# Cached grouped-query attention: scores further ahead of values, K further ahead of V, and weights loaded in row pieces

## The chip, the cores and the metric

The kernel runs on one core of a Trainium2 chip. The metric is the time on the device in microseconds (us), as a median of several runs. Engines are named as in the profile: PE (TensorE, matmuls; its weight loads are PEld), DVE (VectorE), ACT (ScalarE), POOL (GpSimd) and SP (SyncE, which issues nearly all DMAs here). Line numbers (L143) are those of the kernel before, as printed below.

## The reference

Eight sequences with four new tokens each attend to a cache of 2048 positions. There are 32 query heads and 8 key/value heads of 128 elements, so four query heads share one key/value head. All tensors are bf16.

```python
B, Sq, D = 8, 4, 512
Hq, Hkv, Sk, Dh = 32, 8, 2048, 128
q = (x @ wq).reshape(B, Sq, Hq, Dh).transpose(0, 2, 1, 3)
k = jnp.repeat(k_cache, Hq // Hkv, axis=1)
v = jnp.repeat(v_cache, Hq // Hkv, axis=1)
scores = jnp.einsum("bhqd,bhkd->bhqk", q, k) * (Dh ** -0.5)
p = softmax(scores)
o = jnp.einsum("bhqk,bhkd->bhqd", p, v)
return o.transpose(0, 2, 1, 3).reshape(B, Sq, Hq * Dh) @ wo
```

k_cache and v_cache hold 33.6 MB each, wq and wo 4.2 MB each.

## The kernel before

**Units.** The work is cut into 32 units: four pairs of key/value heads (p, outer) times eight sequences (b, inner). A unit needs 1 MB of K and 1 MB of V. Both come as tiles of 128 partitions with 32 chunks of 128 elements; partitions 0 to 63 hold the first head of the pair and 64 to 127 the second. A unit has 32 query columns: eight query heads by four tokens. It is worked on as two halves of 16 chunks, so there are 64 half-units.

**A half-unit's stages.** `transpose_part` (L136 on) turns eight chunks of K with PE against an identity into one PSUM tile `kp`, and DVE copies it to `kt` (ACT in one of four cases). `scores` multiplies 16 chunks of `kt` by the queries into `s_ps`, and ACT writes the exponentials into `probs`, separately for the two heads' partitions; the crossed blocks keep the zeros set at the start. `values` multiplies 16 chunks of V by `probs` into `o_ps`. In the second half of a unit it first sums the probabilities: eight matmuls with `ones` over all 32 chunks into `l_ps` (L178), a reduction on DVE (L186) and a reciprocal (L193); at the end DVE writes `o_ps` times that reciprocal into `oT_all` (L206).

**Reordering and projection.** `shuffle` takes the eight heads of a finished pair, turns them to token order (`nat`), copies, turns them again into the row order in which wo is loaded (`perm`) and copies the result to `oP[p]`. `project` then multiplies `oP` by wo, in two column halves of 256 in two PSUM banks (L270).

**Order.** The order of each engine is the order of the program text (`manual_schedule`); waits are put between engines where data or buffers need them. The loop over steps runs from -2 to 63. Step i does the transposes of half-unit i+2, the scores of i+1 and the values of i. In the first half-unit of a pair's second sequence it also does the whole `shuffle` of the pair before. After a unit's second half the loop issues `load_k(u + 1 + KB)` and `load_v(u + VB)`; K has seven buffers (KB) and V six (VB). The six loads of wo are issued after unit 25's second half, behind the last V. After the loop come `project(0)`, the last `shuffle`, the other projections, two casts (L286, L287) and two stores.

**Loads.** All loads go through SP in the order x, wq (one load of 128 partitions, 32 KB each), K0, K1, V0, K2, V1 and so on: K(u+1) stands directly ahead of V(u). SP holds an issue until the buffer is free and until an earlier load's semaphore can be used again.

Of the kernel before, what the change touches and what calls it, by code (L numbers as in the profile page):

```python
# [7 lines left out]

BF16 = mybir.dt.bfloat16
FP32 = mybir.dt.float32  # L10
EXP = mybir.ActivationFunctionType.Exp


@with_exitstack
def kernel(
# [9 lines left out]
    nc = tc.nc  # L25

    B, Sq, D = x.shape
# [4 lines left out]
    T = B * Sq  # L32
    R = D // 128
    G2 = Hkv // 2
    C = 2 * Sk // 128
    NQ = 2 * rep * Sq
    HC = C // 2
    HP = 2 * rep
    scale = float(Dh) ** -0.5
    NU = G2 * B  # L40
    NH = 2 * NU
    KB = 7
    VB = 6
    WR = HP
    DH = D // 2
    assert Dh == 128 and C == 32 and NQ == 32

    const = ctx.enter_context(tc.tile_pool(name="const", bufs=1))
# [3 lines left out]
    small = ctx.enter_context(tc.tile_pool(name="small", bufs=2))  # L52
    psum_k = ctx.enter_context(tc.tile_pool(name="psum_k", bufs=3, space=bass.MemoryType.PSUM))
    psum_s = ctx.enter_context(tc.tile_pool(name="psum_s", bufs=2, space=bass.MemoryType.PSUM))
    psum_o = ctx.enter_context(tc.tile_pool(name="psum_o", bufs=2, space=bass.MemoryType.PSUM))
    psum_l = ctx.enter_context(tc.tile_pool(name="psum_l", bufs=1, space=bass.MemoryType.PSUM))
# [5 lines left out]
    wq_sb = const.tile([128, R, HqDh], BF16, name="wq_sb")  # L62
    xT_sb = const.tile([128, R, T], BF16, name="xT_sb")
    qT_all = const.tile([128, G2, B, HP, Sq], BF16, name="qT_all")
    oT_all = const.tile([128, Hq, B, Sq], BF16, name="oT_all")
    wo_sb = const.tile([128, G2, WR, D], BF16, name="wo_sb")
    out_sb = [const.tile([T, DH], BF16, name=f"out_sb{i}") for i in range(2)]
    ident = const.tile([128, 128], BF16, name="ident")
    ones = const.tile([128, 128], BF16, name="ones")
    probs = [const.tile([128, C, NQ], BF16, name=f"probs{i}") for i in range(3)]  # L70

    units = [(p, b) for p in range(G2) for b in range(B)]
    ks = [None] * NU
# [2 lines left out]
    def load_k(u):  # L76
        if u >= NU:
            return
        p, b = units[u]
        ks[u] = kpool.tile([128, C, Dh], BF16, tag="k_sb", name="k_sb")  # L80
        nc.sync.dma_start(  # L81
            ks[u][:, :, :],
            k_cache[b, 2 * p : 2 * p + 2].rearrange("g (s c) d -> (g s) c d", c=C),
        )

    def load_v(u):
        if u >= NU:
            return
        p, b = units[u]
        vs[u] = vpool.tile([128, C, Dh], BF16, tag="v_sb", name="v_sb")  # L90
        nc.sync.dma_start(  # L91
            vs[u][:, :, :],
            v_cache[b, 2 * p : 2 * p + 2].rearrange("g (s c) d -> (g s) c d", c=C),
        )

    def load_wo(p, r0, n):
        rows = wo[p * HP * 128 : (p + 1) * HP * 128, :].rearrange("(q r) j -> q r j", r=WR)
        nc.sync.dma_start(wo_sb[:, p, r0 : r0 + n, :], rows[:, r0 : r0 + n, :])

    nc.sync.dma_start(x_sb[:, :], x.flatten_outer_dims())  # L100
    nc.sync.dma_start(wq_sb[:, :, :], wq.rearrange("(p r) n -> p r n", r=R))  # L101
    load_k(0)
    for u in range(VB):
        load_k(u + 1)
        load_v(u)

    make_identity(nc, ident[:])
    nc.vector.memset(ones[:, :], 1.0)
# [9 lines left out]
    for p in range(G2):  # L118
        psq = psum_s.tile([128, HP, T], FP32, tag="s", name="psq")
        for h in range(HP):  # L120
            hh = p * HP + h
            for r in range(R):
# [3 lines left out]
                    rhs=xT_sb[:, r, :],  # L126
# [11 lines left out]
    def transpose_part(i, part):  # L138
        u, hf = divmod(i, 2)
        c0 = hf * HC + part * (HC // 2)  # L140
        kp = psum_k.tile([128, HC // 2, 128], BF16, tag="k", name="kp")
        for c in range(HC // 2):
            nc.tensor.transpose(kp[:, c, :], ks[u][:, c0 + c, :], ident[:, :])  # L143
        k_t = ktpool.tile([128, HC // 2, 128], BF16, tag="kt", name="kt")
        if part == 1 and hf == 1:
            nc.scalar.copy(out=k_t[:, :, :], in_=kp[:, :, :])  # L146
        else:
            nc.vector.tensor_copy(out=k_t[:, :, :], in_=kp[:, :, :])  # L148
        kt[(i, part)] = k_t
# [21 lines left out]
    def values(i):  # L171
        u, hf = divmod(i, 2)
        p, b = units[u]
        pr = probs[u % len(probs)]
        if hf == 1:
            l_ps = psum_l.tile([128, 4, NQ], FP32, tag="l", name="l_ps")
            for c in range(C // 4):
                nc.tensor.matmul(  # L178
                    l_ps[:, :, :],
                    lhsT=ones[:, :],  # L180
                    rhs=pr[:, c * 4 : (c + 1) * 4, :],
                    start=(c == 0),
                    stop=(c == C // 4 - 1),
                )
            l_sb = small.tile([128, NQ], FP32, tag="l_sb", name="l_sb")
            nc.vector.tensor_reduce(  # L186
                out=l_sb[:, :],
                in_=l_ps[:, :, :].rearrange("d c q -> d q c"),
                axis=mybir.AxisListType.X,
                op=mybir.AluOpType.add,  # L190
            )
            r_sb = small.tile([128, NQ], FP32, tag="r_sb", name="r_sb")
            nc.vector.reciprocal(r_sb[:, :], l_sb[:, :])  # L193
        if hf == 0:
            o_ps[u] = psum_o.tile([128, NQ], FP32, tag="o", name="o_ps")
        for c in range(HC):
            cc = hf * HC + c
            nc.tensor.matmul(  # L198
                o_ps[u][:, :],
                lhsT=vs[u][:, cc, :],  # L200
                rhs=pr[:, cc, :],
                start=(cc == 0),
                stop=(cc == C - 1),
            )
        if hf == 1:
            nc.vector.tensor_tensor(  # L206
                out=oT_all[:, p * HP : (p + 1) * HP, b, :],
                in0=o_ps[u][:, :].rearrange("d (h s) -> d h s", h=HP),
                in1=r_sb[:, :].rearrange("d (h s) -> d h s", h=HP),
                op=mybir.AluOpType.mult,  # L210
            )

    oP = [None] * G2

    def shuffle(p):
        nat = psum_l.tile([T, HP, 128], BF16, tag="l", name="nat")
        for h in range(HP):
            nc.tensor.transpose(  # L218
                nat[:, h, :],
                oT_all[:, p * HP + h, :, :].rearrange("d b s -> d (b s)"),  # L220
                ident[:, :],
            )
        nat_sb = small.tile([T, HP * 128 // WR, WR], BF16, tag="nat_sb", name="nat_sb")
        nc.vector.tensor_copy(  # L224
            out=nat_sb[:, :, :].rearrange("t q r -> t (q r)"),
            in_=nat[:, :, :].rearrange("t h d -> t (h d)"),
        )
        perm = psum_l.tile([128, WR, T], BF16, tag="l", name="perm")
        for r in range(WR):
            nc.tensor.transpose(  # L230
                perm[:, r, :],
                nat_sb[:, :, :].rearrange("t q r -> t r q")[:, r, :],
                ident[:T, :T],
            )
        oP[p] = const.tile([128, WR, T], BF16, name=f"oP{p}")
        nc.vector.tensor_copy(out=oP[p][:, :, :], in_=perm[:, :, :])

    for step in range(-2, NH):
        if step + 2 < NH:
            transpose_part(step + 2, 0)  # L240
        if 0 <= step + 1 < NH:
            scores(step + 1)
        if step + 2 < NH:
            transpose_part(step + 2, 1)
        if step < 0:
            continue
        values(step)
        u, hf = divmod(step, 2)
        p, b = units[u]
        if hf == 0:  # L250
            if b == 1 and p > 0:
                shuffle(p - 1)
        else:
            if u == 0:
                load_k(KB)
            load_k(u + 1 + KB)
            load_v(u + VB)
            if u + VB == NU - 1:
                for w in range(G2 - 1):
                    load_wo(w, 0, WR)  # L260
                load_wo(G2 - 1, 0, 4)
                load_wo(G2 - 1, 4, 2)
                load_wo(G2 - 1, 6, 2)

    out_ps = [psum_s.tile([T, DH], FP32, tag="s", name=f"out_ps{i}") for i in range(2)]

    def project(p, r0, n):
        for half in range(2):
            for r in range(r0, r0 + n):
                nc.tensor.matmul(  # L270
                    out_ps[half][:, :],
                    lhsT=oP[p][:, r, :],
                    rhs=wo_sb[:, p, r, half * DH : (half + 1) * DH],
                    start=(p == 0 and r == 0),
                    stop=(p == G2 - 1 and r == WR - 1),
                )

    project(0, 0, WR)
    shuffle(G2 - 1)
    for p in range(1, G2 - 1):  # L280
        project(p, 0, WR)
    project(G2 - 1, 0, 4)
    project(G2 - 1, 4, 2)
    project(G2 - 1, 6, 2)
    o2 = out.flatten_outer_dims()
    nc.vector.tensor_copy(out=out_sb[0][:, :], in_=out_ps[0][:, :])  # L286
    nc.scalar.copy(out=out_sb[1][:, :], in_=out_ps[1][:, :])  # L287
    nc.sync.dma_start(out=o2[:, :DH], in_=out_sb[0][:, :])
    nc.scalar.dma_start(out=o2[:, DH:], in_=out_sb[1][:, :])


# [28 lines left out]
```

## Time and profile before

| | us |
|---|---|
| median of 7 runs | 197.31 |
| lowest, highest | 197.11, 198.26 |
| the profiled run | 196.99 |
| its span in the trace | 195.2 |
| busy in the span: PE, PEld | 152.9, 143.2 |
| busy in the span: DVE, ACT | 97.3, 84.0 |
| HBM read | 75.53 MB, 387 GB/s over the span |
| median time from issue to landing, K and V loads | 20.2 each |

The span is the time between the first and the last instruction in the trace; the run's time holds some 1.8 us more around it. PE and PEld overlap, so their times are not added. A DMA's instruction on SP is short; its bytes move later, and the time to landing is from the issue to the last byte. An issue that lies long in the queue behind others therefore has a long landing time.

### The profile page before, as it was taken

To read this page: it belongs to the slowest core of one execution; us is meant where nothing else is said; L and a number is where in the kernel's file an instruction comes from. 1 tells how busy PE (TensorE), PEld (TensorE's weight loads), DVE (VectorE), ACT (ScalarE), POOL (GpSimd) and SP (SyncE) were. 2 spreads that over 40 slices of the span, in tenths; PEclk is the share of its full clock that TensorE was granted. 3 is DMA by queue.
4 is the path that set the end of the run, shared out by engine and by line. 5 is a ranking of instruction groups with operands and counts; after the bars stand their busy time and mean duration, and the time that the engine had idled before them with its cause. 6 is when DMAs were issued, how large, how long until landed. Compare 5 with 4: busy or idle time off the path is not lost.

```text
span 195.2 us, 7883 instructions
## 1 busy us (share of the span) xinstructions
PE 152.9 (78%) x3588; PEld 143.2 (73%) x3588; DVE 97.3 (50%) x209; ACT 84.0 (43%) x166; POOL 0.7 (0%) x6
## 2 busy tenths in 40 slices
PE   1029887888579869988888789988987798878984
PEld 0029887777479869977777689877877798777873
DVE  4003455555427545655555547655554566545310
ACT  2003654544535515645554535645544265445200
POOL 1000000000000000000000000000000000000000
PEclk9999999999969997999999969999999999999999
DMA  6989999999999999999999999999999999999610
GB/s 222 430 383 430 423 416 418 420 423 413 421 418 420 411 421 421 423 411 420 421 423 413 421 413 425 416 418 415 421 416 418 420 420 416 421 420 408 260 50 7
DMA packets 10401, 76.07 MB, mean 390 GB/s; under 512 B 1184, under 2 KB 1280, under 8 KB 1664
## 3 DMA queue, kind: packets, MB, share of 16 engines
q1 hardware_dynamic: 10320, 75.55, 93.4%
q8 instruction: 28, 0.46, 1.0%
q14 instruction: 5, 0.04, 0.1%
q10 hardware_dynamic: 48, 0.02, 0.0%
HBM read 75.53 MB, written 0.03 MB: 387 GB/s over the span
## 4 chain that ended last, share of the span: by engine, by line
DMA 74%; PE 18%; issue 2%; SPq 1%; ACT 1%; DVE 1%; ACTq 0%
DMA v_sb<-in_v_cache_dram 74%; PE kp L143 6%; PE out_ps L270 4%; PE s_ps L159 3%; PE o_ps L198 3%; PE l_ps L178 2%; DVE nat_sb L224 1%; PE perm L230 1%; SPq L81 1%; PE nat L218 1%; ACT kt L146 1%; ACT probs L165 0%; SPq L91 0%; SPq L101 0%; SPq L100 0%
## 5 line engine op out<-in xcount | busy, mean ns | idle before, releaser
L148 DVE COPY kt<-kp 128x1024 bf16<-128x1024 bf16 x96 | 66.0, 689 | 52.2 <-PE kp L143 42.3
L143 PE MATMUL kp<-ident,k_sb 128*128 128x128 bf16 x1024 | 81.6, 223 | 6.8 <-issue 6.6
L165 ACT ACTIVATE probs<-s_ps 64x256 bf16<-64x256 f32 x128 | 48.4, 378 | 82.3 <-PE s_ps L159 80.8
L143 PEld LDWEIGHTS <-k_sb 128*128 128x128 bf16 x1024 | 60.7, 99 | 8.2 <-issue 7.8
L198 PE MATMUL o_ps<-probs,v_sb 128*128 128x32 bf16 x1024 | 36.1, 177 | 13.9 <-DMA v_sb<-in_v_cache_dram 13.6
L198 PEld LDWEIGHTS <-v_sb 128*128 128x128 bf16 x1024 | 31.8, 96 | 17.5 <-DMA v_sb<-in_v_cache_dram 17.2
L159 PE MATMUL s_ps<-qT_all,kt 128*128 128x32 bf16 x1024 | 39.5, 177 | 2.1 <-ACT kt L146 0.8
L159 PEld LDWEIGHTS <-kt 128*128 128x128 bf16 x1024 | 34.2, 97 | 4.4 <-ACT kt L146 1.1
L146 ACT COPY kt<-kp 128x1024 bf16<-128x1024 bf16 x32 | 32.4, 1012 | 1.7 <-PE kp L143 1.0
L186 DVE TENSOR_REDUCE l_sb<-l_ps 128x32 f32<-128x128 f32 x32 | 9.3, 292 | 24.8 <-PE l_ps L178 24.8
L178 PE MATMUL l_ps<-probs,ones 128*128 128x128 bf16 x256 | 21.3, 228 | 0.6 <-ACT probs L165 0.3
L178 PEld LDWEIGHTS <-ones 128*128 128x128 bf16 x256 | 16.9, 103 | 0.8 <-issue 0.8
L193 DVE RECIPROCAL r_sb<-l_sb 128x32 f32<-128x32 f32 x32 | 11.3, 353 | 1.1
L123 PE MATMUL psq<-xT_sb,wq_sb 128*128 128x32 bf16 x128 | 3.6, 188 | 10.3 <-DMA wq_sb<-in_wq_dram 10.3
L123 PEld LDWEIGHTS <-wq_sb 128*128 128x128 bf16 x128 | 3.5, 104 | 10.4 <-DMA wq_sb<-in_wq_dram 10.4
L206 DVE TENSOR_TENSOR oT_all<-o_ps,r_sb 128x32 bf16<-128x32 f32 x32 | 6.1, 192 | 3.3
L130 ACT ACTIVATE qT_all<-psq 128x256 bf16<-128x256 f32 x4 | 1.5, 385 | 14.0 <-PE psq L123 14.0
L270 PE MATMUL out_ps<-wo_sb,oP 128*32 128x256 bf16 x64 | 7.3, 273 | 0.0
L270 PEld LDWEIGHTS <-oP 128*32 128x32 bf16 x64 | 6.0, 97 | 0.8
L230 PE MATMUL perm<-ident,nat_sb 32*128 32x32 bf16 x32 | 2.7, 212 | 3.1 <-DVE nat_sb L224 3.1
L230 PEld LDWEIGHTS <-nat_sb 32*128 32x128 bf16 x32 | 2.3, 162 | 3.8 <-DVE nat_sb L224 3.8
L224 DVE COPY nat_sb<-nat 32x1024 bf16<-32x1024 bf16 x4 | 2.7, 679 | 4.6 <-PE nat L218 4.6
(17 smaller groups left out, 11.4 us busy)
## 6 DMA issues: line engine op xcount, KB each, us to landing
k_sb<-in_k_cache_dram SPq DMA_DIRECT2D x32, 1024.0 KB, 20.2
v_sb<-in_v_cache_dram SPq DMA_DIRECT2D x32, 1024.0 KB, 20.2
wq_sb<-in_wq_dram SPq DMA_DIRECT2D x1, 4096.0 KB, 12.3
wo_sb<-in_wo_dram SPq DMA_DIRECT2D x3, 1024.0 KB, 21.3
wo_sb<-in_wo_dram SPq DMA_DIRECT2D x1, 512.0 KB, 20.1
wo_sb<-in_wo_dram SPq DMA_DIRECT2D x2, 256.0 KB, 17.3
x_sb<-in_x_dram SPq DMA_DIRECT2D x1, 32.0 KB, 1.7
out_dram<-out_sb SPq DMA_DIRECT2D x1, 16.0 KB, 1.4
```

Source lines behind the costliest of these rows:

```text
L123: nc.tensor.matmul(psq[:, h, :], lhsT=wq_sb[:, r, hh * 128 : (hh + 1) * 128], rhs=xT_sb[:, r, :], start=(r == 0), stop=(r == R - 1),)
L143: nc.tensor.transpose(kp[:, c, :], ks[u][:, c0 + c, :], ident[:, :])
L146: nc.scalar.copy(out=k_t[:, :, :], in_=kp[:, :, :])
L148: nc.vector.tensor_copy(out=k_t[:, :, :], in_=kp[:, :, :])
L159: nc.tensor.matmul(s_ps[:, c, :], lhsT=k_t[:, c % (HC // 2), :], rhs=q2, start=True, stop=True)
L165: nc.scalar.activation(out=pr[rows, hf * HC : (hf + 1) * HC, cols], in_=s_ps[rows, :, cols], func=EXP)
L178: nc.tensor.matmul(l_ps[:, :, :], lhsT=ones[:, :], rhs=pr[:, c * 4 : (c + 1) * 4, :], start=(c == 0), stop=(c == C // 4 - 1),)
L186: nc.vector.tensor_reduce(out=l_sb[:, :], in_=l_ps[:, :, :].rearrange("d c q -> d q c"), axis=mybir.AxisListType.X, op=mybir.AluOpType.add,)
L193: nc.vector.reciprocal(r_sb[:, :], l_sb[:, :])
L198: nc.tensor.matmul(o_ps[u][:, :], lhsT=vs[u][:, cc, :], rhs=pr[:, cc, :], start=(cc == 0), stop=(cc == C - 1),)
L230: nc.tensor.transpose(perm[:, r, :], nat_sb[:, :, :].rearrange("t q r -> t r q")[:, r, :], ident[:T, :T],)
L270: nc.tensor.matmul(out_ps[half][:, :], lhsT=oP[p][:, r, :], rhs=wo_sb[:, p, r, half * DH : (half + 1) * DH], start=(p == 0 and r == 0), st ...
```

## The change

- The loop starts at -7. Step i does the transposes of half-unit i+7, the scores of i+6 and the values of i. `probs` has five buffers, not three.
- The order of loads becomes K0, K1, K2, K3, V0, K4, V1 and so on. A list of loads is walked by `load_ready` after every step, as far as the counts of finished units allow.
- The sums of a unit (`norms`) are made before the second half's values, with two matmuls of 512 columns in place of eight of 128, and a reduction over 16 columns a query in place of four. The final multiplication is a function of its own (`finish`).
- `shuffle` is split: `to_tokens` in the pair's second sequence, `to_wo_rows` in its third. After the loop, `to_tokens(3)` precedes `project(0)` and `to_wo_rows(3)` follows it.
- The projection has one PSUM tile of 512 columns: 32 matmuls in place of 64. Two casts read its halves into one tile, and one store writes the output.
- wq and the first three of the four pairs of wo are each loaded as three DMAs, of partitions 0 to 111, 112 to 119 and 120 to 127.

```diff
+PARTS = [(0, 112), (112, 120), (120, 128)]
...
+    L = 6
+    KA = L // 2 + 1
...
+    LC = 16
...
-    probs = [const.tile([128, C, NQ], BF16, name=f"probs{i}") for i in range(3)]
+    probs = [const.tile([128, C, NQ], BF16, name=f"probs{i}") for i in range(L // 2 + 2)]
...
-        nc.sync.dma_start(wo_sb[:, p, r0 : r0 + n, :], rows[:, r0 : r0 + n, :])
+        for lo, hi in PARTS if n == WR else [(0, 128)]:
+            nc.sync.dma_start(wo_sb[lo:hi, p, r0 : r0 + n, :], rows[lo:hi, r0 : r0 + n, :])
...
-    nc.sync.dma_start(wq_sb[:, :, :], wq.rearrange("(p r) n -> p r n", r=R))
-    load_k(0)
-    for u in range(VB):
-        load_k(u + 1)
-        load_v(u)
+    for lo, hi in PARTS:
+        nc.sync.dma_start(wq_sb[lo:hi, :, :], wq.rearrange("(p r) n -> p r n", r=R)[lo:hi])
+    loads = []
+    for u in range(NU + KA):
+        if u < NU:
+            loads.append(("k", u))
+        if u >= KA - 1 and u - KA + 1 < NU:
+            loads.append(("v", u - KA + 1))
+    loads.reverse()
+
+    def load_ready(nk, nv):
+
+        while loads:
+            kind, u = loads[-1]
+            if u >= (nk + KB if kind == "k" else nv + VB):
+                return
+            loads.pop()
+            (load_k if kind == "k" else load_v)(u)
+
+    load_ready(0, 0)
...
+    def norms(u):
+        pr = probs[u % len(probs)]
+        l_ps = psum_l.tile([128, LC, NQ], FP32, tag="l", name="l_ps")
+        for c in range(0, C, LC):
+            nc.tensor.matmul(
+                l_ps[:, :, :],
+                lhsT=ones[:, :],
+                rhs=pr[:, c : c + LC, :],
+                start=(c == 0),
+                stop=(c + LC == C),
+            )
...
-    for step in range(-2, NH):
-        if step + 2 < NH:
-            transpose_part(step + 2, 0)
-        if 0 <= step + 1 < NH:
-            scores(step + 1)
-        if step + 2 < NH:
-            transpose_part(step + 2, 1)
...
+    for step in range(-L - 1, NH):
+        i, j = step + L + 1, step + L
+        if i < NH:
+            transpose_part(i, 0)
+        if 0 <= j < NH:
+            scores(j)
+        if i < NH:
+            transpose_part(i, 1)
         u, hf = divmod(step, 2)
...
+        if step >= 0:
+            p, b = units[u]
+            if hf == 1:
+                norms(u)
+            values(step)
+            if hf == 1:
+                finish(u)
+            elif p > 0 and b == 1:
+                to_tokens(p - 1)
+            elif p > 0 and b == 2:
+                to_wo_rows(p - 1)
+        load_ready(min((i + 1) // 2, NU), max((step + 1) // 2, 0))
+        if step == NH - 1 - 2 * VB:
+            assert not loads
+            for w in range(G2 - 1):
+                load_wo(w, 0, WR)
+            load_wo(G2 - 1, 0, 4)
+            load_wo(G2 - 1, 4, 2)
+            load_wo(G2 - 1, 6, 2)
...
+        for r in range(r0, r0 + n):
+            nc.tensor.matmul(
+                out_ps[:, :],
+                lhsT=oP[p][:, r, :],
+                rhs=wo_sb[:, p, r, :],
+                start=(p == 0 and r == 0),
+                stop=(p == G2 - 1 and r == WR - 1),
+            )
+
+    to_tokens(G2 - 1)
     project(0, 0, WR)
-    shuffle(G2 - 1)
+    to_wo_rows(G2 - 1)
...
+    nc.vector.tensor_copy(out=out_sb[:, :DH], in_=out_ps[:, :DH])
+    nc.scalar.copy(out=out_sb[:, DH:], in_=out_ps[:, DH:])
+    nc.sync.dma_start(out=out.flatten_outer_dims(), in_=out_sb[:, :])
```

More of the change, by code (lines that the diff above doesn't have):

```diff
@@ L43 @@
     VB = 6
+    L = 6
+    KA = L // 2 + 1
     WR = HP
     DH = D // 2
+    AX = mybir.AxisListType.X
+    LC = 16
+    ADD = mybir.AluOpType.add
     assert Dh == 128 and C == 32 and NQ == 32
@@ L66 @@
     wo_sb = const.tile([128, G2, WR, D], BF16, name="wo_sb")
-    out_sb = [const.tile([T, DH], BF16, name=f"out_sb{i}") for i in range(2)]
+    out_sb = const.tile([T, D], BF16, name="out_sb")
+    oP = [const.tile([128, WR, T], BF16, name=f"oP{p}") for p in range(G2)]
     ident = const.tile([128, 128], BF16, name="ident")
     ones = const.tile([128, 128], BF16, name="ones")
-    probs = [const.tile([128, C, NQ], BF16, name=f"probs{i}") for i in range(3)]
+    probs = [const.tile([128, C, NQ], BF16, name=f"probs{i}") for i in range(L // 2 + 2)]
     units = [(p, b) for p in range(G2) for b in range(B)]
@@ L174, in values @@
         pr = probs[u % len(probs)]
[L175 to L193, printed above, removed]
         if hf == 0:
@@ L204, in values, with finish, to_tokens @@
             )
[L205 to L210, printed above, removed]
-            )
-    oP = [None] * G2
-    def shuffle(p):
+    r_sbs = {}
+    def norms(u):
[8 more added lines that the diff above has]
+                stop=(c + LC == C),
+            )
+        l_sb = small.tile([128, NQ], FP32, tag="l_sb", name="l_sb")
+        nc.vector.tensor_reduce(
+            out=l_sb[:, :], in_=l_ps[:, :, :].rearrange("d c q -> d q c"), axis=AX, op=ADD
+        )
+        r_sb = small.tile([128, NQ], FP32, tag="r_sb", name="r_sb")
+        nc.vector.reciprocal(r_sb[:, :], l_sb[:, :])
+        r_sbs[u] = r_sb
+    def finish(u):
+        p, b = units[u]
+        nc.vector.tensor_tensor(
+            out=oT_all[:, p * HP : (p + 1) * HP, b, :],
+            in0=o_ps[u][:, :].rearrange("d (h s) -> d h s", h=HP),
+            in1=r_sbs[u][:, :].rearrange("d (h s) -> d h s", h=HP),
+            op=mybir.AluOpType.mult,
+        )
+    nats = {}
+    def to_tokens(p):
         nat = psum_l.tile([T, HP, 128], BF16, tag="l", name="nat")
@@ L227, in shuffle, with to_wo_rows @@
         )
+        nats[p] = nat_sb
+    def to_wo_rows(p):
         perm = psum_l.tile([128, WR, T], BF16, tag="l", name="perm")
@@ L231, in shuffle @@
                 perm[:, r, :],
-                nat_sb[:, :, :].rearrange("t q r -> t r q")[:, r, :],
+                nats[p][:, :, :].rearrange("t q r -> t r q")[:, r, :],
                 ident[:T, :T],
             )
-        oP[p] = const.tile([128, WR, T], BF16, name=f"oP{p}")
         nc.vector.tensor_copy(out=oP[p][:, :, :], in_=perm[:, :, :])
-    for step in range(-2, NH):
-        if step + 2 < NH:
-            transpose_part(step + 2, 0)
-        if 0 <= step + 1 < NH:
-            scores(step + 1)
-        if step + 2 < NH:
-            transpose_part(step + 2, 1)
-        if step < 0:
-            continue
-        values(step)
-        u, hf = divmod(step, 2)
[L249 to L263, printed above, removed]
@@ L265 @@
-    out_ps = [psum_s.tile([T, DH], FP32, tag="s", name=f"out_ps{i}") for i in range(2)]
-    def project(p, r0, n):
[L268 to L276, printed above, removed]
+    for step in range(-L - 1, NH):
[6 more added lines that the diff above has]
+            transpose_part(i, 1)
+        u, hf = divmod(step, 2)
+        if step >= 0:
+            p, b = units[u]
+            if hf == 1:
[15 more added lines that the diff above has]
+            load_wo(G2 - 1, 6, 2)
@@ L278 @@
+    out_ps = psum_s.tile([T, D], FP32, tag="s", name="out_ps")
+    def project(p, r0, n):
+        for r in range(r0, r0 + n):
[5 more added lines that the diff above has]
+                stop=(p == G2 - 1 and r == WR - 1),
+            )
+    to_tokens(G2 - 1)
     project(0, 0, WR)
-    shuffle(G2 - 1)
+    to_wo_rows(G2 - 1)
     for p in range(1, G2 - 1):
@@ L284 @@
     project(G2 - 1, 6, 2)
[L285 to L289, printed above, removed]
+    nc.vector.tensor_copy(out=out_sb[:, :DH], in_=out_ps[:, :DH])
+    nc.scalar.copy(out=out_sb[:, DH:], in_=out_ps[:, DH:])
+    nc.sync.dma_start(out=out.flatten_outer_dims(), in_=out_sb[:, :])
 _INS = ['x', 'k_cache', 'v_cache', 'wq', 'wo']
```

## The prediction, made before the changed kernel ran

> **What bounds the kernel now.** I read the page's slices and DMA queues first, because the kernel loads 75.5 MB and computes little with them.
>
> ```profile
> GB/s 222 430 383 430 423 416 418 420 423 413 421 418 420 411 421 421 423 411 420 421 423 413 421 413 425 416 418 415 421 416 418 420 420 416 421 420 408 260 50 7
> q1 hardware_dynamic: 10320, 75.55, 93.4%
> q8 instruction: 28, 0.46, 1.0%
> ```
>
> From the second slice to the 37th the loads run at about 420 GB/s without a hole, then thin out over two slices (260, 50). A table of stretches of the tail (columns: stretch, length, busy us and count of PE, PEld, DVE, ACT, POOL, clock, DMA share, GB/s) shows how:
>
> ```profile
> 152.00:178.00 26.00, 22.55 (x560) 21.48 (x561) 15.61 (x33) 12.84 (x26) 0.00 (x0) 1.00 1.01 419
> 182.00:184.00 2.00, 1.70 (x32) 1.47 (x30) 0.84 (x3) 0.40 (x2) 0.00 (x0) 1.00 0.56 226
> 184.00:186.00 2.00, 1.54 (x19) 1.26 (x16) 0.42 (x1) 0.00 (x0) 0.00 (x0) 1.00 0.49 190
> 186.00:188.50 2.50, 2.18 (x23) 1.99 (x24) 0.55 (x2) 0.00 (x0) 0.00 (x0) 1.00 0.16 57
> 188.50:192.40 3.90, 3.83 (x36) 3.16 (x33) 0.25 (x1) 0.03 (x1) 0.00 (x0) 1.00 0.00 0
> ```
>
> For 4 us half of the 16 DMA engines have nothing left (share 0.56, 0.49). The completion counts in the trace say the same load by load: wq's 16 counts came within 0.28 us of one another, those of the last wo load at 181.8 (first) to 188.3 (last). Eight are within 2.2 us of the first, eight are 4.7 to 6.5 us behind it. The late eight fell back in jumps of about 1.5 us, as many as there are packets on queue q8: instruction blocks, each taking about 1.07 us.
>
> Third, the view of wo's loads and the chain that ended last (start, length, what):
>
> ```profile
> L98 SPq DMA_DIRECT2D wo_sb<-in_wo_dram x6: 327/327/328, 159.5 to 171.9; - x6
> DMA to landing us min/median/max: 16.4/20.7/21.3
> ```
> ```profile
> 151.98 0.05 issue
> ...
> 183.25 1.85 PE out_ps L270 x16
> 185.10 0.46 PE nat L218 x8
> 185.56 0.02 issue
> 185.58 0.69 DVE nat_sb L224
> 186.27 0.05 issue
> 186.32 0.67 PE perm L230 x8
> 186.99 5.36 PE out_ps L270 x48
> 192.34 0.02 issue
> 192.37 0.36 ACT out_sb L287
> ```
>
> The last wo load lands at 171.9 + 16.4 = 188.3, but PE ends the projection at 192.34. From 151.98, where a V landing last released it, to that end, PE waits for no load: it carries transposes, scores and values that could have run earlier. Two things end late: PE 4.0 us after the last byte, and the last byte 6.5 us after the fastest DMA engine.
>
> Fourth, the waits of the load queue:
>
> ```profile
> SPq L81 <- DMA wq_sb<-in_wq_dram: 8.3, 1, 8.3
> ```
>
> The tenth load (K4) was issued at 13.51, when wq, the second, landed: a load waits for the one eight before it, so eight are in flight.
>
> [...] The trace has only loads of 128 rows or 32, all with 16 counts; it shows no 8-row load. [...]
>
> **The change part by part.** One DMA engine moves its 64 KB of a 1 MB load in 2.48 us (V issues in the steady state are 2.48 apart): 25.8 KB per us.
>
> *Schedule.* Scores run six half-units ahead of values instead of one, and K(u+3) is queued just ahead of V(u) where K(u+1) was. Per unit PE's chain pieces are 4 x 0.46 (transposes) + 2 x 0.39 (scores) + 0.45 (sums) + 2 x 0.39 (values) = 3.85 us, and a unit's two loads take 4.96. From 14.7 us on PE has 3.6 (wq product) + 32 x 3.85 + 3 x 1.1 (reorderings) = 130 us of work, so some 33 us of slack before the last V lands at 177.9. When it lands, all transposes and scores are done; PE owes two value groups and a sum, 1.2 us, then nat 0.46, project(0) 1.8, perm 0.67, and the middle pairs at 8 x 0.223 = 1.8 us against 2.48 between landings of wo. PE then waits for wo. After its last landing two matmuls stay. This removes the backlog; what is late next is the last wo byte.
>
> Load queue: V(u+6) needs values(u) finished, which now also follows the first half of K(u+4), landing just after V(u). By the eight-load rule it waits for V(u+2), three landings (7.4 us) after K(u+4), against some 2.5 us of PE work, so 5 us cover it. K(u+10) needs only K(u+3) transposed and has more. If that cover went, each late issue would cost its lateness once. At the start K0 to K3 come before V0; PE does a unit of transposes and scores in 2.6 us, the load in 2.48, so it falls behind by under 1 us and regains it later.
>
> *Row sums:* 8 matmuls of 128 columns become 2 of 512, the same columns, 0.45 us. The reduction reads 512 instead of 128 elements: between 0.29 (no change) and 4 x 0.292 = 1.17 us; I take 0.65: 384 elements more at the 0.95 ns an element that the memset of probs shows (485 ns for 512). It follows no V and finishes beside values; DVE is busy 97 of 195 us. Two more memsets of probs (0.49 each) end before 4 us, under the wait for wq. Cost nothing.
>
> *Reordering split:* the waits of perm for DVE's copy (0.78 each) are filled with a step's other work. Nothing on the path, since PE has slack.
>
> *Projection:* 64 matmuls at 5.36/48 = 0.112 become 32 at 0.223: the same 7.1 us, but only 0.45 after the last landing. Casting two halves of one bank: [...] the casts run between together (0.41) and in turn (0.8); the trace, with two banks, does not show it. I take 0.6. One store of 32 KB instead of two of 16: 1.4 us as now.
>
> *Row pieces:* wq as 112 + 8 + 8 rows gives eight engines nine rows of 32 KB and eight engines seven; three 1 MB loads of wo do so with rows of 8 KB. So 32 + 24 = 56 KB move from one half of the engines to the other: 2.17 us. If the relieved half is the late one, it ends at 6.55 - 2.17 = 4.4 and the other at 2.15 + 2.17 = 4.3: the last byte comes at 188.3 - 2.17 = 186.1. Eight more issues of 0.33 us fit beside the queue's waits. The small loads also take places among the eight in flight: at the end they hold about 1.9 MB, 4.6 us, enough. wq itself ends 1.2 us later, which the slack covers. PE loses 192 + 32 matmuls with their loads, so 6728 instructions, two blocks fewer; I count nothing for that.
>
> *Sum.* 186.1 + 0.1 (release) + 0.45 (two matmuls) + 0.6 (casts) + 2.47 (from the end of ACT's cast at 192.73 to the end of the span, 195.2) = 189.7, that is 5.5 less. The profiled run took 196.99 around its span: 191.5. The median of the seven runs is 0.3 above that run: 191.8; with the terms rounded I take **191.9**. Its own range is 190.5 to 193.5, from the casts, the fetched blocks and a last landing within 1 us.
>
> **The rivals.**
>
> *Relief without effect.* The pieces cost what they save (issue and small transfers), and the last landing stays at 188.3: 2.17 later, 194.1. For it: no run here shows what eight small loads cost the engines beside their bytes. Against: nine rows remain nine rows of time.
>
> *Relief on the wrong half.* If the late eight are mixed among the low numbers, a late engine gets 2.17 more: landing at 190.5, 4.4 after the forecast's, and 196.3, near no change. For it: no view numbers the engines. Against: the late eight form one clean group, as eight neighbours would.
>
> [...]
>
> That the schedule does not do what it says (PE still behind at 178) has 33 us of slack against it; I give it nothing of its own.
>
> **How the numbers follow.** Forecast 0.58; relief without effect 0.10; wrong half 0.07[...]. What 0.3% of 197.3, 0.6 us, cannot tell from no change is only part of the wrong half. Faster 0.58 + 0.10 + 0.04 = 0.72; same 0.03; slower 0.25. The range goes from 190.2 past the second and third case[...] up to 200.5 it leaves 0.2 out.
>
> **What would show it.** Right: the chain ends wo landing, two matmuls of 512 columns, casts; PE waits for wo near the end; the DMA share drops steeply from 1 to 0; scores wait for no V. Wrong: wq landing after 16 us, or a DMA share near 0.5 for several us at the start or the end[...]; SP waiting for PE during the steady state (buffers); PE still without waits after 178.

## The result, and the profile after

The changed kernel takes 219.25 us (median of 12 runs, 218.05 to 220.17); the kernel before took 197.52 beside it. The ratio is 1.110, with a 95% interval of 1.108 to 1.112. The forecast was 191.9 and its range ended at 200.5, so the time lies far outside, on the other side of the kernel before. The span of the profiled run went from 195.2 to 217.4 us. Line numbers from here on are those of the kernel whose view is shown.

The slices of the changed kernel (GB/s in 40 equal slices, here 5.4 us each) and its DMA queues:

```profile
GB/s 199 235 258 128 83 365 422 416 422 421 418 421 414 417 414 422 417 421 419 419 416 424 416 421 422 416 419 411 422 414 427 411 424 411 255 216 219 216 91 8
...
q1 hardware_dynamic: 10384, 75.57, 94.4%
q8 instruction: 26, 0.43, 0.8%
```

The middle is as before, about 418 GB/s. Two stretches are new: five slices at the start with 83 to 258 GB/s, where wq is loaded, and four at the end with 216 to 255, where wo is. The bytes are the same. The table of stretches shows both (columns as in the prediction's: stretch, length, five engines, clock, DMA share, GB/s):

```profile
15.00:20.00 5.00, 0.00 (x0) 0.00 (x0) 0.00 (x0) 0.00 (x0) 0.00 (x0) 1.00 1.04 134
20.00:25.00 5.00, 0.00 (x0) 0.00 (x0) 0.00 (x0) 0.00 (x0) 0.00 (x0) 1.00 0.95 98
...
195.00:200.00 5.00, 2.11 (x43) 1.35 (x39) 1.69 (x4) 0.00 (x0) 0.00 (x0) 0.50 0.95 202
```

The DMA share stays near 1 while 98 GB/s are moved. The DMA engines are not out of work, as half of them were at the end of the kernel before; each packet takes longer. A row of wq, one packet of 32 KB, takes 1.21 us in the trace of the kernel before; here it takes 2.13 in the load of 112 rows (medians) and 3.6 to 5.2 in the two of 8 rows. So of the two signs of trouble at the start or the end that the forecast named, wq's late landing came (28.8 us, and the sign was 16), but the share of 0.5 did not. PE has nothing to do until wq is there. The view of wq shows when its product starts (min/median/max ns, first and last start), 28.9 us where before it was 13.5:

```profile
L147 PE MATMUL psq<-xT_sb,wq_sb x128: 176/188/190, 28.9 to 32.3; 128*128 128x32 bf16 x128
```

The view of wo's loads, now twelve, gives the last landing as 205.5 + 7.3 = 212.8, against 188.3:

```profile
L107 SPq DMA_DIRECT2D wo_sb<-in_wo_dram x12: 271/302/1343, 175.6 to 205.5; - x12
...
DMA to landing us min/median/max: 7.3/15.4/23.5
```

The end of the chain that ended last:

```profile
175.58 26.06 DMA wo_sb<-in_wo_dram
201.64 0.02 issue
201.66 8.78 DMA wo_sb<-in_wo_dram
210.44 0.14 issue
210.57 3.63 PE out_ps L301 x16
214.20 0.02 issue
214.23 0.42 DVE out_sb L317
214.65 0.02 issue
214.67 0.36 ACT out_sb L318
```

As forecast, PE's backlog has left the chain: from 175.6 on it consists of wo's loads, the last 16 matmuls and the casts, with no transpose. But it spends 34.9 us on the loads. ACT's cast also waits for DVE's: it begins at 214.67, when DVE's has ended, while in the kernel before DVE's ran 0.41 us from 192.1 and ACT's began at 192.37. The two now read one PSUM tile and write one output tile; which of these makes ACT wait is not shown.

### The profile page after: what moved, and what is told of

The parts are those of the page before. It is cut to its first block, busy times and chain, and to the rows that moved or that the text cites. A ratio compares the mean times of both kernels' runs of the same rounds, so it can differ in the third digit from the quotient of the medians.

```text
span 217.4 us, 7343 instructions
## 1 busy us (share of the span) xinstructions
PE 150.1 (69%) x3334; PEld 132.1 (61%) x3364; DVE 107.6 (50%) x211; ACT 83.9 (39%) x166; POOL 0.7 (0%) x6
## 4 chain that ended last, share of the span: by engine, by line
DMA 92%; PE 5%; issue 0%; SPq 0%; DVE 0%; ACT 0%
DMA k_sb<-in_k_cache_dram 68%; DMA wo_sb<-in_wo_dram 16%; DMA wq_sb<-in_wq_dram 8%; PE kp L167 2%; PE out_ps L301 2%; PE o_ps L203 1%; PE s_ps L183 1%; PE l_ps L217 0%; PE nat L246 0%; DVE out_sb L317 0%; SPq L109 0%; ACT out_sb L318 0%; SPq L99 0%; SPq L89 0%
## 5 line engine op out<-in xcount | busy, mean ns | idle before, releaser
L167 PE MATMUL kp<-ident,k_sb 128*128 128x128 bf16 x1024 | 79.1, 223 | 16.8 <-DMA k_sb<-in_k_cache_dram 16.8
L167 PEld LDWEIGHTS <-k_sb 128*128 128x128 bf16 x1024 | 59.9, 99 | 19.1 <-DMA k_sb<-in_k_cache_dram 19.0
L203 PEld LDWEIGHTS <-v_sb 128*128 128x128 bf16 x1024 | 34.4, 97 | 16.5 <-DMA v_sb<-in_v_cache_dram 7.2
L183 PE MATMUL s_ps<-qT_all,kt 128*128 128x32 bf16 x1024 | 38.4, 177 | 5.9 <-ACT kt L170 4.9
L225 DVE TENSOR_REDUCE l_sb<-l_ps 128x32 f32<-128x512 f32 x32 | 21.9, 683 | 9.3 <-remote 4.2
L217 PE MATMUL l_ps<-probs,ones 128*128 128x512 bf16 x34 | 13.7, 414 | 1.5 <-issue 0.4
L301 PE MATMUL out_ps<-wo_sb,oP 128*32 128x512 bf16 x32 | 9.0, 437 | 2.8 <-DMA wo_sb<-in_wo_dram 2.8
L301 PEld LDWEIGHTS <-oP 128*32 128x32 bf16 x32 | 3.2, 106 | 7.6 <-DMA wo_sb<-in_wo_dram 3.6
L217 PEld LDWEIGHTS <-ones 128*128 128x128 bf16 x64 | 5.0, 100 | 0.1
L266 DVE COPY oP<-perm 128x256 bf16<-128x256 bf16 x4 | 1.2, 291 | 5.7 <-PE perm L261 5.7
```

The costliest lines, as they stand in the source:

```text
L183: nc.tensor.matmul(s_ps[:, c, :], lhsT=k_t[:, c % (HC // 2), :], rhs=q2, start=True, stop=True)
L203: nc.tensor.matmul(o_ps[u][:, :], lhsT=vs[u][:, cc, :], rhs=pr[:, cc, :], start=(cc == 0), stop=(cc == C - 1),)
L217: nc.tensor.matmul(l_ps[:, :, :], lhsT=ones[:, :], rhs=pr[:, c : c + LC, :], start=(c == 0), stop=(c + LC == C),)
L225: nc.vector.tensor_reduce(out=l_sb[:, :], in_=l_ps[:, :, :].rearrange("d c q -> d q c"), axis=AX, op=ADD)
L301: nc.tensor.matmul(out_ps[:, :], lhsT=oP[p][:, r, :], rhs=wo_sb[:, p, r, :], start=(p == 0 and r == 0), stop=(p == G2 - 1 and r == WR - 1),)
```

## The experiments

The expectations weigh three theories. P: a load into a part of the partitions runs at a lower rate. N: the pieces cost only as far as eight DMA engines carry nine rows and eight carry seven. S: the new schedule costs the time. The nine and seven are in the changed kernel's packet records: the 112 rows post 16 completion counts, and their packets, 2.13 us in the median, run in 16 streams from 2.2 to between 16.1 and 17.6 us, about seven each; a load of 8 rows has eight packets and eight counts, and each packet of the second such load begins 1 to 3 ns after one of the first ends, so the same eight engines take both. The kernel before, run beside each, took 197.2 to 197.5 us.

**Taking the pieces out, and putting them in alone.** First the changed kernel with whole loads:

```diff
-PARTS = [(0, 112), (112, 120), (120, 128)]
+PARTS = [(0, 128)]
```

> The changed kernel with wq and wo in whole loads of 128 rows; all the rest of the change stays. Theory P (the row pieces are slow[...]): the loss goes and the gain of the schedule shows, 193 to 195 us, as the case 'relief without effect' of the prediction worked out (194.1). Theory S (the schedule itself, with V starting later and its new load order, costs the time): still 214 to 219. Theory N (pieces cost only because eight engines carry nine rows): 2 us less than the changed kernel, about 217.

Measured: 196.01 us, ratio to before 0.990 (0.987 to 0.994). The whole loss is in the pieces. The rest of the change gains 1%; at 194.1 the prediction had it 1.9 us faster than this.

Then the pieces on the kernel before (wq and the first three pairs of wo by PARTS, nothing else changed):

```diff
-        nc.sync.dma_start(wo_sb[:, p, r0 : r0 + n, :], rows[:, r0 : r0 + n, :])
+        for lo, hi in PARTS if n == WR else [(0, 128)]:
+            nc.sync.dma_start(wo_sb[lo:hi, p, r0 : r0 + n, :], rows[lo:hi, r0 : r0 + n, :])
...
-    nc.sync.dma_start(wq_sb[:, :, :], wq.rearrange("(p r) n -> p r n", r=R))
+    for lo, hi in PARTS:
+        nc.sync.dma_start(wq_sb[lo:hi, :, :], wq.rearrange("(p r) n -> p r n", r=R)[lo:hi])
```

> The kernel before with only wq and three quarters of wo in pieces of 112, 8 and 8 rows. Theory P: wq lands some 15 us later than 13.5 and wo's loads cost 8 to 10 us more, so 214 to 222 us. Theory S: 197 to 200. Theory N: about 199.

Measured: 219.4 us, 1.110 (1.104 to 1.116), the same as the changed kernel. S is out, as the schedule without pieces takes 196, and so is N, which left some 199 us for this run.

The changed kernel with pieces for wq alone:

```diff
-        for lo, hi in PARTS if n == WR else [(0, 128)]:
+        for lo, hi in [(0, 128)]:
```

> The changed kernel with pieces for wq alone, wo in whole loads. Theory P: the 5.7 MB that the first 32 us lost, at 418 GB/s 13.7 us, come on top of the 194 of whole loads: 206 to 209 us, with wq landing near 29. Theory S or N: within 2 us of the changed kernel, 217 to 219.

Measured: 209.06 us, 1.055 (1.049 to 1.062). And for wo alone:

```diff
-    for lo, hi in PARTS:
+    for lo, hi in [(0, 128)]:
         nc.sync.dma_start(wq_sb[lo:hi, :, :], wq.rearrange("(p r) n -> p r n", r=R)[lo:hi])
```

> The changed kernel with pieces for wo alone, wq in one whole load. Theory P: wq lands near 13.5; the tail from the last V's landing to the last wo byte is some 20 us instead of 10, so 202 to 206 us, and the two losses of wq and wo pieces add up to that of both within 2 us. Theory S or N: 215 to 219.

Measured: 205.06 us, 1.037 (1.030 to 1.045). Over whole loads wq's pieces cost 13.1 us and wo's 9.1, together 22.1 of the 23.2 that both cost. The slices of the two, wq alone first, then wo alone, show each loss in its own place:

```profile
GB/s 202 234 278 130 84 297 419 420 419 422 414 420 420 419 414 419 419 416 422 422 414 420 419 425 412 419 420 417 417 419 419 417 423 417 422 412 420 362 96 6
```
```profile
GB/s 214 414 422 422 427 414 417 425 416 417 419 416 419 422 417 419 417 419 422 417 416 421 421 422 416 417 417 417 419 419 417 422 417 400 210 230 220 210 118 6
```

**Same bytes for every engine.** Two loads of 64 rows, and 112 plus 16 rows, were meant to leave every engine with eight rows of wq (wo whole in both):

```diff
-PARTS = [(0, 112), (112, 120), (120, 128)]
+PARTS = [(0, 64), (64, 128)]
```

> The changed kernel with wo in whole loads and wq as two loads of 64 rows (0 to 63, 64 to 127)[...]. Theory N (uneven bytes on the engines are what costs) and a cost per load: wq lands at 13.5 to 14.5, the time within 1 us of whole loads.

```diff
-PARTS = [(0, 112), (112, 120), (120, 128)]
+PARTS = [(0, 112), (112, 128)]
```

> The changed kernel with wo in whole loads and wq as 112 rows and 16 rows: seven rows and one row for each of 16 engines, so no engine carries more than another. [...] Theory N: wq lands at 13.5 to 14 and the time is that of whole loads, 196.

Measured: 207.16 and 205.13 us in one execution each (whole loads: 195.26 to 196.34). The views of wq give the start of its product, first for 64 + 64, then for 112 + 16:

```profile
L147 PE MATMUL psq<-xT_sb,wq_sb x128: 186/188/189, 24.3 to 27.7; 128*128 128x32 bf16 x128
```
```profile
L147 PE MATMUL psq<-xT_sb,wq_sb x128: 186/188/188, 23.4 to 26.8; 128*128 128x32 bf16 x128
```

By the completion counts in the trace the halves land at 14.1 and 24.2; the 112 rows at 16.8 to 19.1 and the 16 rows at 20.5 to 23.3, where the whole load landed at 13.5 in the kernel before. N is out once more: at 1.21 us a row, being some 10 us late would take an engine with about eight rows more than its eight (an estimate from these landings). So 112 rows are slow by themselves (in the second run their packets already took some 2 us each before the 16 rows began), which the prediction had not priced.

**One extra load of 8 rows.** The pieces come in threes, which hides who slows whom. So one load was added to the kernel with whole loads, behind wq and ahead of K0, with the same 256 KB each time and only the target partitions changed:

```diff
+    extra = wo_sb[112:120].rearrange("p g r d -> p (g r d)").rearrange("p (r n) -> p r n", r=R)
+    nc.sync.dma_start(extra, wq.rearrange("(p r) n -> p r n", r=R)[112:120])
     loads = []
```

> The changed kernel with all loads whole, plus one extra load of 8 rows of wq (256 KB) into partitions 112 to 119 of wo's tile, right behind wq; it is overwritten later and computes nothing. [...] Theory N: [...] it lands near 15 and K0 near 17.4.

With `wo_sb[64:96:4]`:

> The same extra 8-row load, but into partitions 64, 68, ... 92[...]. If it is the number of rows or engines that makes an 8-row load slow[...] it lands as late as with partitions 112 to 119[...].

With `wo_sb[0:32:4]`:

> As the extra 8-row load behind wq in the two runs before it, but into partitions 0, 4, ... 28[...] its 8 KB packets take 309 ns as in whole loads (616 into partitions 64 to 92, 1547 into 112 to 119), it lands 1.3 us after wq, and K0 near 17.4. If the other eight engines did not wait for it, eight of K0's counts still come at 15.3 to 16.2; if all wait, all come after 16.5.

With `wo_sb[4:36:4]`:

> The same with partitions 4, 8, ... 32[...]. If the half rate into partitions 64 to 92[...], the packets take about 616 ns here too; if it came from crossing to the other half, 309 ns.

Measured, in one execution each and in the order above: 200.11, 198.03, 194.41 and 195.51 us. In these loads the trace's packet records are plain: a row of wq is one packet of 32,768 bytes, a row of K one of 8192. (The 616 and 1547 ns that the expectation for 0, 4, ... 28 gives to the extra load are K0's rows in the first two runs.) While the extra load's eight packets run, eight of K0's are in flight: eight engines are on the extra load and the other eight already on K0. The median durations in ns, and the landings in us by the completion counts:

```
target of the 8 rows     32 KB row   K0 row meanwhile   extra lands    K0 lands
(none, whole loads)       1213 ns        309 ns             -         15.3 to 16.2
0, 4, ... 28              1213           309           14.0 to 14.5   15.5 to 17.0
4, 8, ... 32              1213        309 to 319       14.2 to 14.7   15.8 to 17.1
64, 68, ... 92            1959           616           15.4 to 16.0   17.0 to 18.3
112 to 119                4380          1547           18.8 to 19.3   20.1 to 21.6
```

The number of rows is not what makes a load of 8 rows slow: into partitions 0, 4, ... 28 each row takes its usual 1.21 us, and half of K0's counts come as early as without it. Into partitions 112 to 119 a row takes 3.6 times as long, and K0's rows on the other eight engines 5 times as long, though most of them go to other partitions. The stretches of that run and of the one into 0 to 28, in this order:

```profile
14.00:15.00 1.00, 0.00 (x0) 0.00 (x0) 0.00 (x0) 0.00 (x0) 0.00 (x0) 1.00 0.39 33
15.00:16.00 1.00, 0.23 (x8) 0.23 (x9) 0.00 (x0) 0.00 (x0) 0.00 (x0) 1.00 0.59 49
16.00:17.00 1.00, 1.00 (x45) 1.00 (x42) 0.00 (x0) 0.16 (x1) 0.00 (x0) 1.00 0.77 66
```
```profile
14.00:15.00 1.00, 1.00 (x44) 1.00 (x41) 0.00 (x0) 0.33 (x1) 0.00 (x0) 1.00 0.99 418
15.00:16.00 1.00, 1.00 (x45) 1.00 (x42) 0.00 (x0) 0.44 (x2) 0.00 (x0) 1.00 1.03 434
```

The last columns are the point: 33 to 66 GB/s beside 418 to 434. Share and rate count a packet where it starts (the share is 2.45 from 12.00 to 13.00, when the extra load's packets begin), so both read low while long ones run. The extra load's own 256 KB over 4.4 us are 60 GB/s more, so it is some 90 to 130 GB/s that move, still under a third.

The run into 64 to 92 sits between: its rows run at 0.6 of the rate (1959 ns against 1213) and K0's at half (616 against 309). Eight rows with the same spacing run at the full rate in the lower 64 partitions and not in the upper, so neither the number of rows nor their spacing decides alone: it matters which partitions are written. By what mechanism is not shown: the trace does not show which partitions an engine writes, and no run loads 8 neighbouring rows into the lower 64 partitions, which would part the neighbours from the upper half.

**Which engines are late.** One more load of 8 rows behind wo, in the kernel before:

```diff
                 load_wo(G2 - 1, 6, 2)
+                nc.sync.dma_start(probe[:, :], wq[0:8, 0:512])
```

> The kernel before, with one more load of 8 rows of 1 KB behind the last load of wo, into a tile that nothing reads. It posts eight completion counts[...]. If the late eight engines are the upper ones, as the forecast's relief needs, all eight counts come within 2.5 us of the first of wo's last load, near 182 to 184.5. If the late ones are the lower eight, all come at 186 to 189. If they are mixed, the eight counts spread over the whole 6.5 us. The time stays within 0.5 us of before.

Measured: 197.6 us. Its counts come at 181.9, 181.9, 182.1, 182.8, 183.3, 183.8 and twice at 188.0. In the same trace wo's last load counts from 181.7 to 183.6 on the early eight engines and from 186.3 to 188.2 on the late eight. So of the eight engines that take this load of 8 rows, six are early and two are late. The late eight are not the eight that such a load leaves free: what the wrong-half rival feared is true of two engines.

**A version faster than both kernels.** From whole loads; the sums of a unit go into its first half, and PE is kept busy while it waits for the last V:

```diff
-            if hf == 1:
+            if hf == 0:
                 norms(u)
+            if step == NH - 2:
+                warm(u)
             values(step)
...
+    def warm(u):
+        w_ps = psum_k.tile([128, LC, NQ], FP32, tag="k", name="w_ps")
+        for c in range(10):
+            nc.tensor.matmul(
+                w_ps[:, :, :],
+                lhsT=ones[:, :],
+                rhs=probs[u % len(probs)][:, :LC, :],
+                start=True,
+                stop=True,
+            )
```

> Whole loads, and the sums of a unit made in its first half instead of its second, so that at the end only values, the final multiplication and the reordering follow the last V; plus ten matmuls of 512 columns on PE while it waits for the last V, whose result nothing reads, so that its clock stays up. Expected from the trace of whole loads: sums and half-clock transposes and projection leave the chain (1.2 to 2 us), the last wo byte at 188.3 becomes the bound, 194.0 to 195.0 us against 196.0. If PE's tail is not what ends the run, 196.

Measured: 194.48 us over 5 runs, 0.985 (0.983 to 0.988). The reason is in the chains. First whole loads:

```profile
178.36 0.56 PE o_ps L203 x16
178.93 0.45 PE l_ps L217 x2
179.38 0.02 issue
179.40 0.70 DVE l_sb L225
...
180.83 1.04 PE nat L246 x8
181.87 2.85 PE out_ps L301 x8
184.72 0.60 PE perm L261 x8
185.31 5.30 PE out_ps L301 x24
```

Behind the last V's values stand the sums and three steps of DVE, for which PE waits, and then work of PE at half clock: eight matmuls take 2.85 us where the last 24 take 0.221 each. The stretch says so (the third number from the end is the clock):

```profile
182.00:184.00 2.00, 2.00 (x6) 0.76 (x5) 0.59 (x1) 0.00 (x0) 0.00 (x0) 0.50 0.53 214
```

In the new version the clock stays at 1.00, and wo's third pair, landing at 185.8, is what PE waits for:

```profile
164.49 21.32 DMA wo_sb<-in_wo_dram
185.81 0.04 issue
185.85 3.63 PE out_ps L314 x16
```

The two edits were tried together, but one of the runs above bears on their shares. With the extra load into 0 to 28 the sums still followed the last V, no matmuls were added, and the clock stayed at 1.00 by itself:

```profile
182.00:184.00 2.00, 2.00 (x16) 1.07 (x14) 0.35 (x2) 0.00 (x0) 0.00 (x0) 1.00 0.71 279
```
```profile
165.34 20.33 DMA wo_sb<-in_wo_dram
185.67 0.04 issue
185.71 3.63 PE out_ps L303 x16
```

It too waits for wo's third pair and ends at 194.41. In this one execution the full clock alone was worth as much as both edits; what the moved sums add is not shown, nor why the clock stayed.

## Why the prediction was wrong

**The step that failed** is the price of the row pieces. The forecast took a row at 1.24 us whatever partitions it goes to ("nine rows remain nine rows of time", so a net 2.17 us for eight engines) and moved the last landing to 186.1. Measured, a 32 KB row takes 1.21 us in a load of 128 rows, mostly 1.9 to 2.3 in one of 112, about 2.56 in one of 64, and 3.6 to 5.2 in one of 8 neighbouring rows. The pieces cost 23.2 us instead of gaining.

**The case of slow pieces was set too low, at 0.25, and reached too short.** What it took for a piece was not shown by any trace: the kernel before has no load of 8 rows. Measured, the two 8-row pieces of wq add 4.9 and 4.5 us (counts complete at 19.4, 24.3 and 28.8). Two terms were missing. It took the load of 112 rows at full rate; in the changed kernel this landed at 19.4 where the whole wq, with more bytes, lands at 13.7. And it charged only the eight engines that take the 8-row pieces, with 4.4 us of room to the late ones; the extra load into 112 to 119 shows that the others slow down with them (K0's rows 1547 ns against 309), so that room cannot be counted on. The argument against the case, that other transfers run beside, was no evidence.

Two loads of 64 rows run at about half the rate of one of 128 (2.56 us a row against 1.21), and 112 rows come to little more than half of it. Why, is not settled.

**Relief could not have worked as placed.** Of the eight engines that take a load of 8 rows, six are early and two late in the run that shows it, so two late ones would have got more to carry. And the rows moved to them are those of partitions 112 to 127: a row into 112 to 119 took 4380 ns in the extra load against 1213, and eight spread rows among 64 to 92 still took 1959. The size of the late group was read rightly from the completion counts. Its place was not known: that eight are late together was no sign that they are neighbours. One count was misread as well: wq's 16 counts lie within 0.52 us of one another (12.98 to 13.50), and 0.28 is the spread of x's.

**The schedule's part held in direction and was mis-sized.** With whole loads the last byte lands at 188.3, as taken over from before, and PE no longer carries transposes to the end. Forecast for that case was 194.1, measured 196.01. The terms: "two matmuls" after the last landing was 0.45, but PE was busy with 24 matmuls of 5.30 us that began at 185.31. Between the last V's landing and these the prediction had 4.1 us (1.2, 0.46, 1.8 and 0.67), and it took 7.0, from 178.32 to 185.31. PE stood idle for 1.1 us while DVE reduced, inverted and multiplied, steps priced at nothing because the reduction "follows no V"; at the end it does. The eight turns (1.04 against 0.46) and project(0) (2.85 against 1.8) ran at half clock. The casts came to 0.8, the upper bound, since they run in turn (DVE from 190.63, ACT from 191.08). With sums first and the clock kept, 194.48 is within 0.4 of the forecast for that case, but partly by chance: the bound there is wo's third pair at 185.8 and 16 matmuls behind it, where the forecast had the last landing at 188.3 and two.

**What held:** the sums and the longer reduction (0.68 us, taken as 0.65) were off the path in the steady state, and PE had its slack. The new order of loads left no hole in the load rate, though the queue waited for PE's values for up to 2.3 us with whole loads and 3.1 in the changed kernel, which the forecast had named as a sign of trouble; other loads were in flight meanwhile.

## What to carry to other kernels

Splitting a load by rows changes which partitions it writes at one time, and that can cost more than the balance it buys (here 23.2 us, for 2.17 that were hoped for): measure the piece by itself, ahead of a transfer whose speed is known, and see what becomes of that transfer too. Moving bytes from late to early DMA engines pays only if it is known which they are; a tiny load's completion counts tell it for the engines that the load uses. When an earlier backlog is removed from the end of a kernel, PE may wait there, so price the remaining chain at a reduced clock too: here it was 0.50 in one run and 1.00 in another.

## What the runs showed of the hardware

- A load into partitions 112 to 119 slowed the DMA engines that did not take part: rows of K0 on the other eight took 1547 ns instead of 309. By what path is not seen.
- Loads of eight rows beside K0 run at full rate into partitions 0, 4, ... 28 and 4, 8, ... 32, and at six tenths of it into 64, 68, ... 92 (1213 and 1959 ns a row).
- Eight of 16 DMA engines end 4.2 to 6.6 us later than the first, in every kernel with whole loads of wo here. In the trace of the kernel before, the last of a load's 16 counts comes 0.52 us after the first for wq, 1.9 once three to eight blocks of instructions have been fetched beside the loads (packets on q8), 3.5 with ten to sixteen, 5.1 with 19 to 24 and 6.5 at the end, with 28; that the blocks cause it is not shown. With 26 blocks instead of 28 it is no smaller at the end (6.39 us with whole loads, 6.52 in the kernel before).
